# Windowed attention with an MLP on one core: shared places for the early pairs, a modelled short transfer queue, and GpSimd waits on VectorE

## The chip, the core and the metric

One of the eight cores of a Trainium2 chip. A core has TensorE (PE: matmuls into PSUM), VectorE (DVE), ScalarE (ACT), GpSimd (POOL), SyncE (SP, which issues the DMAs here) and 16 DMA engines. The metric is the device time of one execution in microseconds. Three runs of the kernel before took 712.12, 712.63 and 714.5 us, so their median is 712.63.

## The reference

```python
# q, k, v: 4 batches x 8 heads x 768 x 64; n_global 8, n_local 96
scores = q @ k.T / 8
rel = i - j;  local = (0 <= rel < n_local);  globl = j < n_global
dist = where(globl & ~local, n_local, abs(rel))
scores = where(local | globl, scores - slope[head] * dist, -1e9)
a = softmax(scores);  x = (a @ v), heads side by side     # 3072 x 512
h = x @ w_in                                              # 512 x 2048
out = (h * cos(h)) @ w_out                                # 2048 x 512
```

Inputs are float32, but the two weight matrices arrive as 64-bit floats, twice as many bytes.

## The kernel before, in words

**Tiles.** The 3072 tokens are 8 chunks of 384 (`CW`). Attention goes by chunk and pair of heads: 32 units, each with one transfer of queries and keys (`raw`), one of values (`v`, in two DMAs), score matmuls, folds and minima on VectorE (lines 538, 547), exponentials on ScalarE (572), sums and reciprocals (580, 583), norms (595, 600), transposes on TensorE (664), masks into `pv` (672, 677) and the product with the values (699), whose result is split into a high and a low part `xh`, `xl` (720). The first 8 units (`EXACT`) score in float32 straight from `raw`; the others split queries and keys into two parts each (`qs`, `ks`: lines 619, 623, 257 or 255, 632). The running extreme of the scores is kept by line 563.

**MLP.** It has 128 steps, one for each chunk and each of 16 slices of 128 hidden columns. A step has 12 matmuls (735), the angle and cosine (752 on ScalarE, 755 on VectorE, 758 on ScalarE), the product h*cos(h) (793), its split into `gh` and `gl` (253, 255 or 257; 802), and nine matmuls of the second product (746). The steps run in the order of `PHASES`: chunk 0 with slices 0 to 7, chunk 1 with all 16, chunk 0 with slices 8 to 15, then the other chunks.

**Weights.** Each of the 32 slices of 512 KB is turned from 64-bit to 32-bit floats once: low word (378 or 380), sign (385 on VectorE or 388 on GpSimd), bias (394 or 396), join (399, VectorE), high part (`w`), rest (409). Many of these may run on one of two or three engines.

**Order.** A planner (`Plan.run`) writes out the order of all engines ahead of time. Each operation has a list of engines with a cost in ns, the operations that it comes after, the places (`Slot`) that it uses, and a due time. The planner steps through its own time, gives each free engine the ready operation with the earliest due time whose places are free, and so fixes engine, order and buffer of each. Each engine then executes its instructions in this order. Two things of its model matter here. GpSimd's operations and those of VectorE marked `port=True` (among them 385, 399, 409, 563, 580, 583, 595, 600, 623, 632, 802 and the copies) hold one common port (`self.port`), so in the plan they never overlap; folds, minima and reads of PSUM aren't marked. Nothing in the emitted program holds an engine to its turn at the port: an instruction waits for its data and places alone. The other is SyncE, which issues a transfer 0.47 us after the last one, however many are still under way; the time of the transfers is modelled as one queue (`dma`), in which each starts behind the last.

**Places.** A class of places is a list of buffer names (`tt` 5, `st` 3, `v` 3, `pv` 3, `raw` 3, `qk` 2). The place of a split pair, `qk`, is a pair of tiles `q0`, `k0` or `q1`, `k1`, in use from the ninth unit on.

**Fillers.** In `emit`, matmuls of zeros (1039) fill planned gaps of TensorE up to 45 us.

Of the kernel before, what the change touches and what calls it, by code (L numbers as in the profile page):

```python
# [10 lines left out]
F32 = mybir.dt.float32  # L11
# [40 lines left out]
PIECES = {-1: [(0, 128), (128, 384)]}  # L52
NT, NST, NPV, NX, NV, NRAW, NQK, NRR, NG = 5, 3, 3, 2, 3, 3, 2, 3, 2

EXACT = 8

FILL_TO, FILL_REST, FILL_EACH, FILL_FIRST, FILL_COLD = 45000, 150, 250, 10, 7000
# [29 lines left out]
class Plan:  # L87
# [38 lines left out]
    def run(self):  # L126
# [19 lines left out]
        while todo:  # L146
# [5 lines left out]
            while again:  # L152
                again = False
                for e, f in self.free.items():
# [55 lines left out]
                    if e == SP:  # L210
                        dma = max(end + 300, dma) + o.extra
                        end = dma + 1400
                    out.append(o)
# [19 lines left out]
class Net:  # L233
# [26 lines left out]
    def constants(self):  # L260
# [7 lines left out]
        make_identity(nc, self.ident)  # L268
        tile3 = lambda name, **kw: self.const.tile([R, 3, SLOT], F32, name=name, **kw)


        self.dd = tile3("dd")
        self.tmp = [tile3(f"tmp{i}", tag=f"tt{i}") for i in range(3)]
        rel, col, _ = self.tmp
# [148 lines left out]
    def plan_loads(self, n, b2):  # L423
# [6 lines left out]
        lead = 1 if c == 0 else 0  # L430
        vs = Slot("v", lambda i: self.work.tile([SLOT, 1 + CT, W], F32, name="v", tag=i))
        L = dict(n=n, first=c == 0, v=vs)
# [18 lines left out]
    def chain(self, name, o):  # L451

        prev = self.prev.get(name)
        if prev is not None:
            o.after.append(prev)
            prev.then.append(o)
            o.left += 1
        self.prev[name] = o
        return o

    def bank(self, cls="att"):
        return Slot(cls, lambda i: self.psum.tile([P, 512], F32, name="bank", tag=i))

    def plan_unit(self, L, pr):
# [13 lines left out]
        if exact:  # L478
# [14 lines left out]
            ready = [p.op({ACT: 520, DVE: 300, POOL: 490}, queries, [o], [raw], port=True)]  # L493
            heads = [(raw, ready)] * 2
        else:
# [4 lines left out]
        st = u["st"] = Slot("st", lambda i: self.work.tile([R, 6 * CT], F32, name="st", tag=i))  # L500
        tt = u["tt"] = [Slot("tt", lambda i: self.const.tile([R, 2, 2, SLOT], F32, name="tt", tag=i)) for _ in range(0, CT, 2)]
        lead = lambda t: first and t == 0
# [4 lines left out]
        for js, h in [(js, h) for js in (((0, 1),) if exact else ((0,), (1,))) for h in range(0, CT, 2)]:  # L507
# [4 lines left out]
            def score(e, ts=ts, pss=pss):  # L512
                for i, t in enumerate(ts):
# [3 lines left out]
                    for j, ps in pss.items():  # L517
                        out = ps.tile[:R, i * WIN : i * WIN + w]
                        if exact:
                            z = raw.tile[j * D : (j + 1) * D]  # L520
                            nc.tensor.matmul(out, z[:, KW:][:, q0], z[:, k : k + w], start=True, stop=True)
                            continue
                        qs, ks = heads[j][0].tile
                        for m in range(2):
# [5 lines left out]
                {PE: cost}, score, [o for j in js for o in heads[j][1]],  # L530
                list(pss.values()) + [heads[j][0] for j in js[:1]] + [st, tt[h // 2]], mode="rows" if exact else None,
            ))
# [74 lines left out]
    def plan_split(self, raw, src, k0, sc):  # L607

        nc, p, D = self.nc, self.plan, self.D
        qk = Slot("qk", lambda i: [  # L610
            self.work.tile([P, 2, CW], F32R, name="qs", tag=f"q{i}"),
            self.work.tile([P, KW], F32R, name="ks", tag=f"k{i}"),
        ])

# [3 lines left out]
        def qhigh(e):  # L618
            nc.scalar.activation(qk.tile[0][:, 0], raw.tile[:, KW:], AF.Copy, scale=sc)

        def qrest(e):
            qs = qk.tile[0]
            nc.vector.scalar_tensor_tensor(  # L623
                qs[:, 1], raw.tile[:, KW:], sc, qs.bitcast(F32)[:, 0], op0=ALU.mult, op1=ALU.subtract
            )

        def khigh(e):
            self.copy(e, qk.tile[1][:, k0:], raw.tile[:, k0:KW])

        def krest(e):  # L630
            ks = qk.tile[1]
# [6 lines left out]
        q = self.chain("qhigh", p.op({ACT: 410}, qhigh, loads, [raw, qk]))  # L638
        q = p.op({DVE: 470}, qrest, [q], [raw, qk], port=True)
        k = self.chain("khigh", p.op(  # L640
            {ACT: 50 + w * 427 // 512, DVE: 70 + w * 265 // 512, POOL: 100 + w * 490 // 512},
            khigh, loads, [raw, qk], port=True,
        ))
        k = p.op({DVE: 70 + w * 535 // 512, POOL: 100 + w * 1125 // 512}, krest, [k], [raw, qk], port=True)
        return qk, [q, k]

    def plan_values(self, u):
# [5 lines left out]
        for h in range(0, CT, 2):  # L653
            pt = self.bank(att)

            pv = Slot("pv", lambda i: self.work.tile([P, 2, 4 * R], F32, name="pv", tag=i))
            lead = u["first"] and h == 0
# [331 lines left out]
    def windows(self):  # L989
# [7 lines left out]
                "px": banks[6:8], "early": banks[5:8] + banks[0:5], "pxearly": banks[6:8] + banks[2:5],  # L997
                "tt": names("tt", NT), "st": names("st", NST), "qk": names("qk", NQK), "raw": names("raw", NRAW),
                "v": names("v", NV), "pv": names("pv", NPV), "x": names("x", NX),
                "rr": names("rr", NRR), "gg": names("gg", NG), "wu": names("wu", 2), "part": names("part", NTOK),  # L1000
# [22 lines left out]
    def emit(self, ops, banks):  # L1023
# [3 lines left out]
        for u in {id(u): u for o in ops for u in o.uses if u.at in held}.values():  # L1027
            held[u.at].append((u.begin, u.end))
        last = 0
        for o in ops:  # L1030
            if o.engine == PE and o.start < FILL_TO:
# [67 lines left out]
```

## Time and profile before

| | us |
|---|---|
| median of the runs | 712.63 |
| the profiled execution: time | 714.17 |
| its span in the trace | 712.4 |
| TensorE matmul busy | 688.6 (97%) |
| VectorE busy | 518.8 (73%) |
| ScalarE busy | 450.9 (63%) |
| GpSimd busy | 135.8 (19%) |

Shares over the span hide that it has two parts. In the first 100 us or so the weights are brought in and converted beside the attention of two chunks; then TensorE works almost without a stop up to 705 us. Busy time of TensorE includes fillers. Busy time of VectorE includes time in which an instruction that has started waits for something that the profile doesn't show. The names DVE, ACT, POOL, PE and SP in rows are those of the engines above; `raw`, `wu` and `w` with 128x512 are weights, `tt` and `st` scores and their statistics.

### The profile page before, as it was taken

What the parts mean: (1) busy time and instruction counts of PE and PEld (TensorE: products, weight loads), DVE (VectorE), ACT (ScalarE), POOL (GpSimd) and SP (SyncE); (2) the same over time, 40 slices, a digit from 0 to 9 for tenths busy, and PEclk for the clock granted to TensorE, in tenths of its full rate; (3) what the DMA queues carried; (4) which work ended last, traced back from release to release, by engine and by line L of the source; (5) the groups of instructions that cost most, each with busy time, mean ns of one, the idle gap of its engine ahead of it and who ended that gap; (6) DMA issues with size and microseconds to landing.
All of it is one profiled execution on the core that took longest, in us unless ns stands there. A gap on an engine that the chain in (4) does not pass through costs nothing.

```text
span 712.4 us, 12947 instructions
## 1 busy us (share of the span) xinstructions
PE 688.6 (97%) x4483; PEld 598.4 (84%) x4483; DVE 518.8 (73%) x1542; ACT 450.9 (63%) x1130; POOL 135.8 (19%) x166
## 2 busy tenths in 40 slices
PE   7898999999999999999999999999999999999996
PEld 3657878988888888889889898888888888899884
DVE  7999999898767778487775887667785877743332
ACT  5799977786756576466664667566764666634342
POOL 4715656530002121011000121011000112000000
PEclk8999999999999999999999999999999999999999
DMA  8997210022420322132230422203122310001001
GB/s 303 407 351 209 59 48 24 1 59 64 112 68 29 83 65 65 48 103 60 56 71 15 112 61 58 59 19 106 42 68 67 90 49 2 1 1 45 1 0 50
DMA packets 32603, 55.74 MB, mean 78 GB/s; under 512 B 3472, under 2 KB 18192, under 8 KB 32528
## 3 DMA queue, kind: packets, MB, share of 16 engines
q1 hardware_dynamic: 32528, 54.82, 26.4%
q8 instruction: 37, 0.61, 0.4%
q14 instruction: 38, 0.31, 0.1%
HBM read 48.52 MB, written 6.29 MB: 77 GB/s over the span
## 4 chain that ended last, share of the span: by engine, by line
PE 72%; DVE 11%; ACT 8%; issue 2%; DMA 1%; POOL 0%; ACTq 0%; DVEq 0%; POOLq 0%; SPq 0%
PE bank L735 31%; PE bank L746 30%; PE bank L699 5%; PE bank L525 3%; ACT tt L572 2%; PE bank L664 2%; DVE wu L399 1%; ACT rr L758 1%; ACT L572 1%; DVE w L409 1%; DVE tt L547 1%; DVE gl L802 1%; DVE rr L755 1%; DVE qs L623 1%; DMA raw<-in_qk_dram 1%
## 5 line engine op out<-in xcount | busy, mean ns | idle before, releaser
L735 PE MATMUL bank<-xh,w 128*128 128x384 f32 x1024 | 298.1, 343 | 4.3 <-DVE rr L793 4.3
L746 PE MATMUL bank<-w,gh 128*128 128x512 f32 x768 | 243.6, 398 | 0.0
L735 PEld LDWEIGHTS bank<-xh,w 128*128 128x128 f32 x1024 | 189.1, 189 | 12.0 <-DVE rr L793 5.8
L735 PE MATMUL bank<-xl,w 128*128 128x384 f32 x512 | 173.3, 339 | 0.8 <-DVE xl L720 0.8
L746 PEld LDWEIGHTS bank<-w,gh 128*128 128x128 f32 x768 | 138.4, 188 | 21.5 <-ACT raw L394 0.3
L746 PE MATMUL bank<-w,gl 128*128 128x512 f32 x384 | 151.9, 396 | 0.0
L755 DVE SCALAR_TENSOR_TENSOR rr<-rr,bank 128x384 f32<-128x384 int32 x129 | 69.8, 542 | 102.6 <-ACT rr L752 102.2
L752 ACT ACTIVATE rr<-bank 128x384 int32<-128x384 f32 x129 | 62.1, 482 | 127.5 <-PE bank L735 124.5
L758 ACT ACTIVATE rr<-rr,half_pi 128x384 f32<-128x384 f32 x129 | 78.4, 613 | 43.0 <-DVE rr L755 41.4
L735 PEld LDWEIGHTS bank<-xl,w 128*128 128x128 f32 x512 | 96.8, 189 | 5.4 <-DVE xl L720 1.4
L793 DVE TENSOR_TENSOR rr<-bank,rr 128x384 f32<-128x384 f32 x129 | 70.5, 551 | 41.2 <-ACT rr L758 40.6
L572 ACT ACTIVATE tt<-tt,st 96x104 f32<-96x104 f32 (+1 forms) x256 | 94.2, 369 | 7.0 <-DVE st L547 6.4
L746 PEld LDWEIGHTS bank<-w,gl 128*128 128x128 f32 x384 | 72.1, 188 | 16.7
L257 POOL TENSOR_SCALAR ks<-raw 128x408 fp32r<-128x408 f32 (+1 forms) x35 | 21.1, 602 | 308.6 <-PE bank L525 291.6
L802 DVE TENSOR_TENSOR gl<-rr,gh 128x384 fp32r<-128x384 f32 (+1 forms) x113 | 65.9, 583 | 7.7 <-ACT gh L253 5.5
L253 ACT CAST gh<-rr 128x384 fp32r<-128x384 f32 (+1 forms) x99 | 50.2, 508 | 29.0 <-DVE rr L793 20.5
L547 DVE CUSTOM_DVE_ANT_0 tt<-bank,dd 96x104 f32<-96x104 f32 (+1 forms) x256 | 55.7, 257 | 3.0
L699 PEld LDWEIGHTS bank<-pv,v 104*64 104x64 f32 (+1 forms) x960 | 42.1, 138 | 12.5 <-issue 8.0
L525 PEld LDWEIGHTS bank<-ks,qs 128*96 128x96 f32 x384 | 45.8, 162 | 5.3 <-issue 0.8
L699 PE MATMUL bank<-pv,v 104*64 104x96 f32 (+1 forms) x960 | 48.3, 252 | 0.8 <-DMA raw<-in_qk_dram 0.4
L525 PE MATMUL bank<-ks,qs 128*96 128x200 f32 (+1 forms) x384 | 47.9, 255 | 0.5 <-DVE st L547 0.5
L572 ACT ACTIVATION_READ_ACCUMULATOR tt<-tt,st 96x1 f32 x256 | 47.9, 187 | 0.0
(96 smaller groups left out, 727.0 us busy)
## 6 DMA issues: line engine op xcount, KB each, us to landing
raw<-in_qk_dram SPq DMA_DIRECT2D x48, 224.0 KB
raw<-in_qk_dram SPq DMA_DIRECT2D x48, 198.0 KB
raw<-in_w_in_dram SPq DMA_DIRECT2D x16, 512.0 KB
raw<-in_w_out_dram SPq DMA_DIRECT2D x16, 512.0 KB
out_dram<-oo SPq DMA_DIRECT2D x24, 256.0 KB
v<-in_v_dram SPq DMA_DIRECT2D x16, 240.0 KB
v<-in_v_dram SPq DMA_DIRECT2D x16, 192.0 KB
raw<-in_qk_dram SPq DMA_DIRECT2D x4, 448.0 KB
```

The lines of the kernel that those rows point to most:

```text
L253: self.nc.scalar.copy(out, x)
L525: nc.tensor.matmul(out, qs[:, m, q0], ks[:, k : k + w], start=m == 0, stop=m == 1)
L547: nc.vector.tensor_tensor_reduce(tt[t // 2].tile[:, t % 2, j, :w], ps.tile[:R, i * WIN : i * WIN + w], self.dd[:, v, :w], op0=ALU.add, op1 ...
L572: nc.scalar.activation(x, x, AF.Exp, bias=st.tile[:, c : c + 1], scale=-1.0, accum_out=st.tile[:, n2 + c : n2 + c + 1])
L699: nc.tensor.matmul(px.tile[j * D : (j + 1) * D, t * R : (t + 1) * R], vs.tile[:k, t + c, hs][:, j * D : (j + 1) * D], pv[:k, c, o : o + R] ...
L735: self.nc.tensor.matmul(ph[:, :CW], self.wi[f][:, w, kk * P : (kk + 1) * P], xx[:, kk, :], start=kk == 0 and m == 0, stop=kk == self.NK - ...
L746: self.nc.tensor.matmul(po, gg[:, ts], self.wo[f][:, w, :], start=start and m == 0, stop=stop and m == 2)
L752: self.nc.scalar.activation(r.bitcast(I32), ph, AF.Copy, scale=1.0 / TWO_PI, bias=0.25)
L755: self.nc.vector.scalar_tensor_tensor(r, r.bitcast(I32), -TWO_PI, ph, op0=ALU.mult, op1=ALU.add)
L758: self.nc.scalar.activation(r, r, AF.Sin, bias=self.half_pi)
L793: {DVE: dve}, lambda e, r=r, h=h: nc.vector.tensor_tensor(r(), h(), r(), op=ALU.mult), [o], [ph, rr]
L802: self.eng(e).tensor_tensor(g[1][:, cs], r(), g[0].bitcast(F32)[:, cs], op=ALU.subtract)
```

## The change

Four edits, all in the planner and what it is given, with some counts:

1. The first seven units (`HOMES`) take `tt`, `v` and `pv` from longer lists of places: `ttearly` has `k0` and `k1` besides, `vearly` has `q0`, `pvearly` has `q1`. For that the pair of tiles `qk` becomes two classes, `q` and `k`. `NST` goes from 3 to 5.
2. In the plan SyncE is free for the next transfer only when the modelled queue is at most `DEPTH` = 3000 ns ahead. The program has no such wait; it changes which transfer is chosen next, and so the order.
3. In `emit`, the first GpSimd operation behind a port operation of VectorE (in the order of the plan) gets a dependency on the last instruction of that operation.
4. The tiles `tmp` and `tt` come from another pool, with the same names and sizes.

```diff
-NT, NST, NPV, NX, NV, NRAW, NQK, NRR, NG = 5, 3, 3, 2, 3, 3, 2, 3, 2
+NT, NST, NPV, NX, NV, NRAW, NQK, NRR, NG = 5, 5, 3, 2, 3, 3, 2, 3, 2
+
+DEPTH = 3000
...
+HOMES = 7
...
                     if e == SP:
                         dma = max(end + 300, dma) + o.extra
+
+                        self.free[SP] = max(end, dma - DEPTH)
+                        heapq.heappush(heap, self.free[SP])
                         end = dma + 1400
...
-        vs = Slot("v", lambda i: self.work.tile([SLOT, 1 + CT, W], F32, name="v", tag=i))
+        vs = Slot(self.early("v", n, b2), lambda i: self.work.tile([SLOT, 1 + CT, W], F32, name="v", tag=i))
...
+    def early(self, cls, n, pr):
+
+        return f"{cls}early" if n * self.NP + pr < HOMES else cls
...
-        tt = u["tt"] = [Slot("tt", lambda i: self.const.tile([R, 2, 2, SLOT], F32, name="tt", tag=i)) for _ in range(0, CT, 2)]
+        tt = u["tt"] = [
+            Slot(self.early("tt", n, pr), lambda i: self.work.tile([R, 2, 2, SLOT], F32, name="tt", tag=i))
+            for _ in range(0, CT, 2)
+        ]
...
-        qk = Slot("qk", lambda i: [
-            self.work.tile([P, 2, CW], F32R, name="qs", tag=f"q{i}"),
-            self.work.tile([P, KW], F32R, name="ks", tag=f"k{i}"),
-        ])
+        qq = Slot("q", lambda i: self.work.tile([P, 2, CW], F32R, name="qs", tag=i))
+        kk = Slot("k", lambda i: self.work.tile([P, KW], F32R, name="ks", tag=i))
...
-            pv = Slot("pv", lambda i: self.work.tile([P, 2, 4 * R], F32, name="pv", tag=i))
+            pv = Slot(self.early("pv", n, pr), lambda i: self.work.tile([P, 2, 4 * R], F32, name="pv", tag=i))
...
-                "v": names("v", NV), "pv": names("pv", NPV), "x": names("x", NX),
+                "v": names("v", NV), "pv": names("pv", NPV), "ttearly": names("tt", NT) + names("k", 2),
+                "vearly": names("v", NV) + ["q0"], "pvearly": names("pv", NPV) + ["q1"], "x": names("x", NX),
...
+        held_by = None
+        behind = mybir.DependencyInfo(mybir.DependencyClass.Sync, mybir.DependencyReason.SCHED_ONLY)
         for o in ops:
...
+            new = len(nc.cur_bb.bb.instructions)
             o.emit(o.engine)
+            if o.engine in (DVE, POOL):
+                engine = self.eng(o.engine).engine
+                new = [i for i in nc.cur_bb.bb.instructions[new:] if i.engine == engine]
+                if o.engine == DVE and o.port:
+                    held_by = new[-1]
+                elif o.engine == POOL and held_by is not None:
+                    self.tc.add_manual_dep(new[0], held_by.name, behind, reason="port")
+                    held_by = None
```

Lines of the changed kernel are numbered 6 to 13 higher from the planner on (399 is 405, 600 is 613, 755 is 766).

GpSimd, at its first conversions of weights, with buffer numbers (`raw_120` to `raw_124` are weights, `tt_258` and `tt_326` scores of the second and third unit) and the semaphores that each row waits for. Before:

```order
32 L380 TENSOR_SCALAR raw_120<-raw_120 128x512 [waits DMAHW1_49]
33 L388 TENSOR_SCALAR raw_120<-raw_120 128x512 [waits Pool_49]
34 L595 TENSOR_TENSOR tt_258<-tt_258,st_259 96x2x96 [waits DVE_49,Activation_49]
35 L595 TENSOR_TENSOR tt_258<-tt_258,st_259 96x208 [waits Activation_49]
36 L388 TENSOR_SCALAR raw_122<-raw_122 128x512 [waits DMAHW3_49,Activation_49]
37 L380 TENSOR_SCALAR raw_124<-raw_124 128x512 [waits DMAHW4_49]
38 L490 TENSOR_SCALAR raw_229<-raw_229,steep_104 128x384 [waits DMAHW6_49,PE_49]
39 L388 TENSOR_SCALAR raw_124<-raw_124 128x512 [waits Pool_49]
40 L396 TENSOR_SCALAR raw_124<-raw_124 128x512 [waits Pool_49]
```

After:

```order
32 L386 TENSOR_SCALAR raw_120<-raw_120 128x512 [waits DMAHW1_49,DVE_49]
33 L394 TENSOR_SCALAR raw_120<-raw_120 128x512 [waits Pool_49]
34 L608 TENSOR_TENSOR tt_258<-tt_258,st_259 96x2x96 [waits DVE_49,Activation_49]
35 L608 TENSOR_TENSOR tt_258<-tt_258,st_259 96x208 [waits Activation_49]
36 L386 TENSOR_SCALAR raw_122<-raw_122 128x512 [waits DMAHW6_49,DVE_49]
37 L394 TENSOR_SCALAR raw_122<-raw_122 128x512 [waits Pool_49]
38 L402 TENSOR_SCALAR raw_122<-raw_122 128x512 [waits Pool_49]
39 L608 TENSOR_TENSOR tt_326<-tt_326,st_327 96x2x96 [waits DVE_49,Activation_49]
40 L608 TENSOR_TENSOR tt_326<-tt_326,st_327 96x208 [waits Activation_49]
41 L394 TENSOR_SCALAR raw_124<-raw_124 128x512 [waits DMAHW7_49,DVE_49,Activation_49]
```

The rows that follow VectorE's port operations have gained `DVE_49`, VectorE's semaphore; the norms of the third unit have come to GpSimd, and the conversions are in another order.

SyncE, where the values of the fourth unit stand. Before (the first row of `v` is theirs):

```order
18 L372 DMA raw<-in_w_in_dram 128x1024
19 L372 DMA raw<-in_w_out_dram 128x1024
20 L372 DMA raw<-in_w_in_dram 128x1024
21 L372 DMA raw<-in_w_out_dram 128x1024 x3
22 L483 DMA raw<-in_qk_dram 128x896
23 L372 DMA raw<-in_w_out_dram 128x1024
24 L372 DMA raw<-in_w_in_dram 128x1024 x2
25 L438 DMA v<-in_v_dram 96x4x128
26 L441 DMA v<-in_v_dram 8x3x128
```

After (the second `v` of 96 rows is theirs):

```order
7 L444 DMA v<-in_v_dram 96x4x128
8 L378 DMA raw<-in_w_in_dram 128x1024
9 L493 DMA raw<-in_qk_dram 128x792
10 L447 DMA v<-in_v_dram 8x3x128
11 L444 DMA v<-in_v_dram 96x4x128
12 L447 DMA v<-in_v_dram 8x3x128
13 L378 DMA raw<-in_w_in_dram 128x1024 x3
14 L378 DMA raw<-in_w_out_dram 128x1024
15 L493 DMA raw<-in_qk_dram 128x896
```

The values and the next queries and keys have moved ahead of the weights; weights and transfers of units now alternate all the way.

VectorE, ahead of its first angle. Before:

```order
170 L563 TENSOR_TENSOR worst<-worst,st 96x8
171 L385 TENSOR_SCALAR raw<-raw 128x512
172 L720 TENSOR_TENSOR xl<-bank,xh 128x384
173 L538 COPY_PREDICATED bank<-mine,bank 96x2x96
174 L672 TENSOR_TENSOR pv<-bank,others 104x384
175 L677 TENSOR_TENSOR pv<-bank,own 96x384
176 L538 COPY_PREDICATED bank<-mine,bank 96x2x96
177 L755 SCALAR_TENSOR_TENSOR rr<-rr,bank 128x384
```

After:

```order
134 L560 ISA tt,st<-bank,dd 96x104
135 L560 ISA st 96x1
136 L415 TENSOR_TENSOR w<-wu,w 128x512
137 L405 SCALAR_TENSOR_TENSOR wu<-raw 128x512
138 L766 SCALAR_TENSOR_TENSOR rr<-rr,bank 128x384
139 L551 COPY_PREDICATED bank<-mine,bank 96x2x96 x2
```

The first angle has moved from row 177 to row 138; weights (415, 405) stand right ahead of it where masks of another unit (672, 677) stood.

## Rows read from the trace of the kernel before

**Rows 1.** Windows: stretch, length, busy us (instructions) of each engine, granted clock, DMA.

```profile
10.00:57.00 47.00, 37.16 (x288) 23.63 (x289) 45.53 (x171) 38.73 (x122) 21.28 (x22) 0.93 1.04 385
57.00:100.00 43.00, 42.94 (x325) 36.21 (x326) 40.62 (x109) 38.72 (x92) 27.53 (x24) 0.96 0.33 83
155.00:600.00 445.00, 441.91 (x2945) 393.50 (x2944) 327.37 (x1019) 282.02 (x721) 51.44 (x64) 1.00 0.24 63
```

**Rows 2.** Windows, filler matmuls of line 1039 alone.

```profile
10.00:57.00 47.00, 13.90 (x55) 5.01 (x55) 0.93 1.04 385
```

**Rows 3.** Timeline of VectorE at the ninth angle: start, us, what.

```profile
104.40 1.01 DVE L755 SCALAR_TENSOR_TENSOR rr<-rr,bank 128x384 f32<-128x384 int32 x2
```

**Rows 4.** Groups of VectorE by form, 10 to 100 us: busy us, mean ns.

```profile
L399 DVE SCALAR_TENSOR_TENSOR wu<-raw 128x512 uint32<-128x512 uint32 x17 | 12.8, 762 | 0.0
L600 DVE TENSOR_TENSOR tt<-tt,st 96x416 f32<-96x416 f32 x11 | 9.6, 892 | 0.0
L409 DVE TENSOR_TENSOR w<-wu,w 128x512 fp32r<-128x512 f32 x10 | 7.6, 765 | 0.0
L563 DVE TENSOR_TENSOR worst<-worst,st 96x8 f32<-96x8 f32 x8 | 3.3, 409 | 0.0
L580 DVE TENSOR_SCALAR st<-st 96x8 f32<-96x8 f32 x8 | 2.9, 367 | 0.6 <-ACT tt L572 0.5
```

**Rows 5.** Lines of VectorE: durations ns min/median/max (409 over the whole span).

```profile
L399 DVE SCALAR_TENSOR_TENSOR wu<-raw x17: 673/681/1550, 24.7 to 97.3; 128x512 uint32<-128x512 uint32 x17
L600 DVE TENSOR_TENSOR tt<-tt,st x11: 575/580/1746, 12.3 to 93.6; 96x416 f32<-96x416 f32 x11
L409 DVE TENSOR_TENSOR w<-wu,w x17: 656/678/1572, 31.3 to 155.3; 128x512 fp32r<-128x512 f32 x17
L563 DVE TENSOR_TENSOR worst<-worst,st x8: 111/262/1039, 17.7 to 89.9; 96x8 f32<-96x8 f32 x8
L580 DVE TENSOR_SCALAR st<-st x8: 156/206/720, 10.8 to 91.4; 96x8 f32<-96x8 f32 x8
```

**Rows 6.** Timeline of GpSimd and VectorE at 12 us.

```profile
12.20 1.33 POOL L388 TENSOR_SCALAR raw<-raw 128x512 bf16<-128x512 bf16 x1
12.27 1.44 DVE L600 TENSOR_TENSOR tt<-tt,st 96x416 f32<-96x416 f32 x1
```

**Rows 7.** Timeline of VectorE and GpSimd at 86 us: a wait of GpSimd.

```profile
85.69 0.68 DVE L399 SCALAR_TENSOR_TENSOR wu<-raw 128x512 uint32<-128x512 uint32 x1
86.45 0.62 POOL L257 TENSOR_SCALAR w<-wu 128x512 fp32r<-128x512 f32 x1 [0.85 <-DVE wu L399]
```

**Rows 8.** Timeline of SyncE and TensorE, 28 to 57 us.

```profile
28.70 0.33 SPq L438 DMA_DIRECT2D v<-in_v_dram  x1
39.32 1.31 PE L521 MATMUL bank<-raw 64*96 64x200 f32 x8
48.99 1.39 PE L699 MATMUL bank<-pv,v 96*64 96x96 f32 x28
56.84 0.44 PE L735 MATMUL bank<-xh,w 128*128 128x384 f32 x1 [3.70 <-DVE rr L793]
```

**Rows 9.** Timeline of VectorE, 36 to 41 us: from start to start.

```profile
36.20 0.74 DVE L385 TENSOR_SCALAR raw<-raw 128x512 uint16<-128x512 uint16 x1
36.73 0.58 DVE L720 TENSOR_TENSOR xl<-bank,xh 128x384 fp32r<-128x384 f32 x1
39.59 1.28 DVE L399 SCALAR_TENSOR_TENSOR wu<-raw 128x512 uint32<-128x512 uint32 x2
```

**Rows 10.** Timeline of VectorE and GpSimd at 313 us.

```profile
313.13 1.84 DVE L623 SCALAR_TENSOR_TENSOR qs<-raw,qs 128x384 fp32r<-128x384 f32 x2
313.50 1.06 POOL L802 TENSOR_TENSOR gl<-rr,gh 128x384 fp32r<-128x384 f32 x1 [4.17 <-ACT gh L253]
```

**Rows 11.** Line 623 over the span.

```profile
L623 DVE SCALAR_TENSOR_TENSOR qs<-raw,qs x48: 520/546/1372, 103.3 to 599.2; 128x384 fp32r<-128x384 f32 x48
```

**Rows 12.** Waits of SyncE's queue, 0 to 110 us: us in total, times, longest.

```profile
SPq L616 <- DVE qs L623: 45.0, 3, 38.6
```

More of the change, by code (lines that the diff above doesn't have):

```diff
@@ L268, in constants @@
         make_identity(nc, self.ident)
-        tile3 = lambda name, **kw: self.const.tile([R, 3, SLOT], F32, name=name, **kw)
-        self.dd = tile3("dd")
-        self.tmp = [tile3(f"tmp{i}", tag=f"tt{i}") for i in range(3)]
+        self.dd = self.const.tile([R, 3, SLOT], F32, name="dd")
+        self.tmp = [self.work.tile([R, 3, SLOT], F32, name=f"tmp{i}", tag=f"tt{i}") for i in range(3)]
         rel, col, _ = self.tmp
@@ L493, in plan_unit @@
             ready = [p.op({ACT: 520, DVE: 300, POOL: 490}, queries, [o], [raw], port=True)]
-            heads = [(raw, ready)] * 2
+            heads = [([raw], ready)] * 2
         else:
@@ L522, in score @@
                             continue
-                        qs, ks = heads[j][0].tile
+                        qs, ks = [x.tile for x in heads[j][0]]
                         for m in range(2):
@@ L530, in plan_unit @@
                 {PE: cost}, score, [o for j in js for o in heads[j][1]],
-                list(pss.values()) + [heads[j][0] for j in js[:1]] + [st, tt[h // 2]], mode="rows" if exact else None,
+                list(pss.values()) + heads[js[0]][0] + [st, tt[h // 2]], mode="rows" if exact else None,
             ))
@@ L618, in qhigh @@
         def qhigh(e):
-            nc.scalar.activation(qk.tile[0][:, 0], raw.tile[:, KW:], AF.Copy, scale=sc)
+            nc.scalar.activation(qq.tile[:, 0], raw.tile[:, KW:], AF.Copy, scale=sc)
         def qrest(e):
-            qs = qk.tile[0]
+            qs = qq.tile
             nc.vector.scalar_tensor_tensor(
@@ L627, in khigh @@
         def khigh(e):
-            self.copy(e, qk.tile[1][:, k0:], raw.tile[:, k0:KW])
+            self.copy(e, kk.tile[:, k0:], raw.tile[:, k0:KW])
         def krest(e):
-            ks = qk.tile[1]
+            ks = kk.tile
             self.eng(e).tensor_tensor(
@@ L637, in plan_split @@
         w = KW - k0
-        q = self.chain("qhigh", p.op({ACT: 410}, qhigh, loads, [raw, qk]))
-        q = p.op({DVE: 470}, qrest, [q], [raw, qk], port=True)
+        q = self.chain("qhigh", p.op({ACT: 410}, qhigh, loads, [raw, qq]))
+        q = p.op({DVE: 470}, qrest, [q], [raw, qq], port=True)
         k = self.chain("khigh", p.op(
             {ACT: 50 + w * 427 // 512, DVE: 70 + w * 265 // 512, POOL: 100 + w * 490 // 512},
-            khigh, loads, [raw, qk], port=True,
+            khigh, loads, [raw, kk], port=True,
         ))
-        k = p.op({DVE: 70 + w * 535 // 512, POOL: 100 + w * 1125 // 512}, krest, [k], [raw, qk], port=True)
-        return qk, [q, k]
+        k = p.op({DVE: 70 + w * 535 // 512, POOL: 100 + w * 1125 // 512}, krest, [k], [raw, kk], port=True)
+        return [qq, kk], [q, k]
     def plan_values(self, u):
@@ L997, in windows @@
                 "px": banks[6:8], "early": banks[5:8] + banks[0:5], "pxearly": banks[6:8] + banks[2:5],
-                "tt": names("tt", NT), "st": names("st", NST), "qk": names("qk", NQK), "raw": names("raw", NRAW),
-                "v": names("v", NV), "pv": names("pv", NPV), "x": names("x", NX),
+                "tt": names("tt", NT), "st": names("st", NST), "q": names("q", NQK), "k": names("k", NQK), "raw": names("raw", NRAW),
+                "v": names("v", NV), "pv": names("pv", NPV), "ttearly": names("tt", NT) + names("k", 2),
+                "vearly": names("v", NV) + ["q0"], "pvearly": names("pv", NPV) + ["q1"], "x": names("x", NX),
                 "rr": names("rr", NRR), "gg": names("gg", NG), "wu": names("wu", 2), "part": names("part", NTOK),
```

## The prediction

> **What bounds the kernel now.** I read the stretches first. They give each engine's busy time in five parts of the span, and the reader is to see that the limit changes. From 155 to 600 us TensorE is busy 441.91 of 445 us and VectorE 327.37; nothing but TensorE's own work can be shortened there, apart from a few stops. From 10 to 57 us TensorE is busy 37.16 of 47 us, while VectorE is busy 45.53, and from 57 to 100 us VectorE still has 40.62 of 43 [rows 1]. TensorE's 37.16 us hold 13.90 us of the filler matmuls of line 1039 [rows 2], so 23.3 of those 47 us are work and 23.7 us are free. The DMA engines are full in the first of these stretches too (385 GB/s, against 83 in the second), but VectorE is idle for only 1.5 us of it, so it is not kept waiting by them. The engine that the others wait for in the ramp is VectorE. It reaches the ninth angle (line 755, the first step of the second chunk) at 104.40 us [rows 3] with 3.9 us of idle since 10 us.
>
> Next I read VectorE's groups by form for 10 to 100 us, beside the quiet length of the same instructions. They say that VectorE's busy time is partly waiting: the mean of line 399 is 762 ns against a median of 681, of line 600 892 against 580, of line 409 765 against 678, of line 563 409 against a shortest of 111, of line 580 367 against 156 [rows 4, 5]. Over their counts that is 17x81 + 11x312 + 10x87 + 8x298 + 8x211 ns = 1.4 + 3.4 + 0.9 + 2.4 + 1.7 = 9.8 us. The timeline shows what does it: a VectorE norm of line 600 that starts at 12.27 takes 1.44 us, because GpSimd's line 388 has started at 12.20 and takes 1.33 [rows 6]. An operation of 0.1 us (line 563) can lose 0.9 us in this way.
>
> **The GpSimd waits.** The order shows 89 of GpSimd's 147 instructions behind a VectorE semaphore, where it was 41 of 133. The planner never lets two port operations overlap, so a VectorE port operation that stretches over a GpSimd one met a GpSimd operation that ran ahead of its place, or stood behind one that was planned before it. VectorE has hardly any idle time in the ramp, which a planned wait for the port would have left room for, and GpSimd is busy only 21.28 of 47 us [rows 1], so it is the one that runs ahead. I expect most of the 9.8 us to go. What comes instead: a GpSimd operation that waits starts 0.08 us after VectorE's end (line 399 ends at 86.37, line 257 starts at 86.45 [rows 7]), and queued behind it on GpSimd stand the other conversions of weights, for which ScalarE and then VectorE's joins (line 399) wait. If each of the 46 GpSimd operations between 10 and 100 us [rows 1] passes that 0.08 us on to VectorE, the waits cost 3.7 us and remove nothing; if the stretching goes wholly and hidden lateness costs nothing, they give 9.8. I take 7, nearer to the row of the stretches, since GpSimd has idle time to absorb lateness.
>
> On the collision itself the row says that VectorE's norm ended at 13.71, 0.18 us behind GpSimd's end at 13.53 [rows 6]. The Trainium skill (SBUF — State Buffer, section "Who interferes with whom") says that an operation which finds the shared port taken blocks fully until the holder is done, and that issue order decides who blocks. By full blocking the norm would have ended at 13.53 + 0.58 = 14.11; the trace has 0.4 us less, so I go by the measured stretches. That issue order decides agrees with the rows, and it also speaks against the change: it is the second rival below.
>
> **The places and the order of transfers.** The order moves the values of the fourth pair. Before, SyncE issued them at 28.70 us, its products on TensorE (line 699) came at 48.99 us, and the third step's matmuls started only at 56.84, after 3.7 us of idle that a VectorE multiplication (line 793) ended [rows 8]. After, that transfer stands behind one weight transfer instead of 18, and the first angle of VectorE (766, was 755) stands at row 138 instead of 177. So the first chunk's steps start earlier, and the free 23.7 us of TensorE begin to fill. But VectorE must do the steps' work instead of something else, so I count what lies ahead of the ninth angle in both orders: four fewer of line 385, three fewer of line 399, and ten small differences more. With the pace from start to start (line 385: 36.20 to 36.73, so 0.53; line 399: two in 1.28 us of which one is 0.68, so 0.60 [rows 9]) the first two are 4x0.53 + 3x0.60 = 3.9 us, and all differences together 5.8. The four conversions go to GpSimd, where each takes about 1.33 us [rows 6], with room for it. None of this work is gone: the weights come later in VectorE's order, at a time in which TensorE has become the limit. I therefore take 2.5 of the 5.8, with bounds of 0 and 5.8. The extra places (tt, v, pv in those of the split pairs; two more st) add no instruction. The number of fillers falls from 65 to 30, which removes nothing that waits.
>
> **The steady stretch.** At 313.13 us two operations of line 623 take 1.84 us, of which GpSimd's line 802, started at 313.50, causes the second one's length of 1.37 [rows 10]; the median of the line is 0.55, the longest 1.37 [rows 11]. The pattern occurs three times with over 0.8 us (146.81, 313.6, 480.4). TensorE is already the limit there and gets the score's queries late. With the wait behind the second 623 this loss of 3x0.82 = 2.5 us can go; I take 2.0, bounds 0 and 2.5.
>
> **The sum.** 7 + 2.5 + 2.0 = 11.5 us. The profiled execution took 714.17 us (span 712.4), so it would take 702.7; it stands 1.54 over the median of the runs shown, 712.63. The forecast for the median is 701.1. The bounds are +3.7 - 0 - 0, which is 716.3, and -9.8 - 5.8 - 2.5 = -18.1, which is 694.5. TensorE's 23.7 free us leave room for the largest gain.
>
> **Rivals.**
> 1. The stretches only change sides. VectorE's next operation starts as its predecessor ends, 0.08 us before the waiting GpSimd sees it [rows 7], and takes the port again; GpSimd comes late, and VectorE's joins then wait for the weights of GpSimd. For it: the many back-to-back port operations in the ramp. Against it: between them stand the folds, minima and PSUM reads (lines 538, 547, 672, 677, 755, 793), which aren't marked as port operations and give GpSimd its turn. Then the first term is about 0 and the rest 4.5: 708.1.
> 2. GpSimd becomes the chain. By issue order GpSimd loses every turn it has waited for, and 24 operations between 57 and 100 us, with 27.53 us of busy time [rows 1], each come one VectorE operation (0.5 us) late: 12 us, which eat the whole 11.5. Then the time is that of before, 713. GpSimd's idle time speaks against it.
> 3. Slower: SyncE's queue. Now 20 of the 32 weight transfers stand behind the transfer of the eighth pair, which needs the place that the fifth pair's second scoring frees. Before, a transfer of this kind waited 38.6 us, with no weight behind it [rows 12]. In before that scoring is not done until 40.6 us [rows 8]; issued at 41, 20x512 KB at 385 GB/s [rows 1] take 27 us and land up to 68 us, where the full stretch ended at 57 [rows 1]. If VectorE, which takes its instructions in order, comes to their joins first, it idles for those 11 us, and for some 4 more where the later transfers of queries and values, which stand between the weights, wait for their places: 15 us against the 11.5 of the gain, so 716. It decides if VectorE idles over 12 us between 35 and 80 us. Against it: those weights are joined late in the new order, and steps of the second half of the weights start after 120 us.
> 4. More than forecast: all three terms at their upper bounds, 694.5, if VectorE's order really is the only limit of the ramp.
>
> **How the numbers follow.** The forecast gets 0.62, rival 1 0.20, rival 2 0.05, rival 3 0.08, rival 4 0.05. The forecast's own range is 697 to 706. I take 694 to 710, which holds the forecast, rival 4 and most of rival 1, and leaves out rivals 2 and 3 and some of rival 1's side above 710. About 0.3% (2.1 us) is what a measurement of this kernel can tell from no change. Faster by more: 0.62 + 0.20 + 0.05 = 0.87; the same: 0.05; slower: 0.08.
>
> **What would show it.** In the profile after, lines 576, 593, 613, 405 (were 563, 580, 600, 399) between 10 and 100 us have means within 0.1 us of the quiet lengths; GpSimd's waits name VectorE; VectorE's ninth angle (766) starts 8 to 12 us before 104.40; line 634 (623) has no length over 1 us at the places in the steady stretch; and the fourth group of values on TensorE (line 710) comes before 38 us. The forecast is wrong if the ninth angle comes at 100 us or later, if VectorE is idle for over 8 us between 10 and 80 us, or if TensorE after 155 us has more idle time than the 3.1 us of now.

## The result, and the profile after

The changed kernel takes 705.59 us (median of 4 runs, 704.92 to 706.55) against 712.38 for the kernel before beside it (4 runs). The ratio is 0.990, 95% interval 0.9876 to 0.9924: a gain of 7.1 us by the ratio and 6.8 by the medians, where 11.5 were forecast. A later repetition gave 0.9901 (0.9878 to 0.9925). The two profiled executions are 714.17 and 704.92 us, a long one of the kernel before and the shortest of the changed kernel, so their difference of 9.2 us holds about 2 us of chance.

Windows of the changed kernel, with the columns of [rows 1]:

```profile
10.00:57.00 47.00, 40.83 (x329) 30.22 (x328) 43.67 (x182) 41.18 (x133) 26.41 (x28) 0.89 0.95 310
57.00:100.00 43.00, 38.19 (x283) 32.43 (x283) 40.40 (x99) 41.40 (x92) 25.94 (x23) 1.00 0.56 168
155.00:600.00 445.00, 442.74 (x2961) 393.65 (x2960) 324.48 (x999) 277.59 (x701) 52.09 (x68) 1.00 0.24 63
```

And the fillers (line 1054, was 1039) in the first stretch:

```profile
10.00:57.00 47.00, 5.00 (x20) 1.70 (x20) 0.89 0.95 310
```

TensorE's 40.83 us hold 5.00 of fillers, so it is busy with work for 35.8 us between 10 and 57 us where it was for 23.3 [rows 1, 2], at a mean granted clock of 0.89 instead of 0.93. It is idle for 4.8 us in the second stretch, where it had no idle time to speak of: the work has been drawn forward, and some of what was won is given back there. Between 155 and 600 us it is idle for 2.3 us (3.1 before). VectorE is idle for 5.9 us between 10 and 100 us, where it was for 3.9.

Groups of VectorE by form between 10 and 100 us, as in [rows 4], with one line more:

```profile
L405 DVE SCALAR_TENSOR_TENSOR wu<-raw 128x512 uint32<-128x512 uint32 x18 | 12.8, 719 | 0.0
L415 DVE TENSOR_TENSOR w<-wu,w 128x512 fp32r<-128x512 f32 x13 | 10.9, 835 | 0.3 <-ACT w L260 0.2
L613 DVE TENSOR_TENSOR tt<-tt,st 96x416 f32<-96x416 f32 x11 | 6.9, 649 | 0.0
L593 DVE TENSOR_SCALAR st<-st 96x8 f32<-96x8 f32 x8 | 2.0, 248 | 0.3 <-ACT tt L585 0.3
L576 DVE TENSOR_TENSOR worst<-worst,st 96x8 f32<-96x8 f32 x8 | 1.5, 183 | 0.0
L813 DVE TENSOR_TENSOR gl<-rr,gh 128x384 fp32r<-128x384 f32 x7 | 5.5, 788 | 0.2 <-ACT gh L260 0.2
```

The quiet lengths over the whole span (columns as in [rows 5]; 593 and 576 have their shortest at 156 and 110 ns):

```profile
L405 DVE SCALAR_TENSOR_TENSOR wu<-raw x32: 633/680/1372, 26.9 to 153.5; 128x512 uint32<-128x512 uint32 x32
L415 DVE TENSOR_TENSOR w<-wu,w x19: 673/693/1342, 28.6 to 152.6; 128x512 fp32r<-128x512 f32 x19
L613 DVE TENSOR_TENSOR tt<-tt,st x39: 577/581/1135, 11.5 to 604.9; 96x416 f32<-96x416 f32 x39
```

By the sum of the prediction (count times mean less quiet length) the five forms now lose to stretches (time beyond the quiet length) 18x39 + 13x142 + 11x68 + 8x92 + 8x73 ns = 4.6 us, where they lost 9.8. So 5.2 us went; in the trace of the repetition (f0 below) the same sum is 5.5, so about 1 us of this is chance. The sum leaves out line 813 (was 802), whose median over the span is 558 ns: it loses 1.6 us now and lost 0.8 before, in this line:

```profile
L802 DVE TENSOR_TENSOR gl<-rr,gh 128x384 fp32r<-128x384 f32 x4 | 3.0, 758 | 0.2 <-ACT gh L253 0.2
```

GpSimd's waits between 10 and 100 us (what waited, for whom: us in total, times, longest):

```profile
POOL raw L394 <- DVE wu L405: 7.3, 4, 2.6
POOL raw L394 <- DVE w L415: 5.3, 4, 2.4
POOL raw L386 <- DVE tt L613: 4.5, 2, 4.0
```

The longest of them name VectorE's port operations. On VectorE's timeline the ninth angle (second row) and the one before it:

```profile
87.97 0.56 DVE L766 SCALAR_TENSOR_TENSOR rr<-rr,bank 128x384 f32<-128x384 int32 x1
90.58 0.54 DVE L766 SCALAR_TENSOR_TENSOR rr<-rr,bank 128x384 f32<-128x384 int32 x1
```

The ninth comes 13.8 us before that of [rows 3]. On TensorE's timeline the values of the fourth unit (line 710, was 699), 18.2 us before theirs in [rows 8]:

```profile
30.80 1.43 PE L710 MATMUL bank<-pv,v 96*64 96x96 f32 x26
```

From the 13th step on, the first matmuls of a step stand 8.6 to 10.5 us apart in the two traces, mostly 9.0 to 10.0, and 9.3 at the last step. So the ninth angle's 13.8 us were not all kept, and the long steady stretch added nothing.

### The profile page after: what moved, and what is told of

Same layout as the page of the kernel before. It is cut to its first block, busy times and chain, and to the rows that moved or that the text cites. A ratio compares the mean times of both kernels' runs of the same rounds, so it can differ in the third digit from the quotient of the medians.

```text
span 703.2 us, 12932 instructions
## 1 busy us (share of the span) xinstructions
PE 681.4 (97%) x4448; PEld 595.5 (85%) x4448; DVE 506.0 (72%) x1531; ACT 450.2 (64%) x1129; POOL 140.1 (20%) x180
## 5 line engine op out<-in xcount | busy, mean ns | idle before, releaser
L813 DVE TENSOR_TENSOR gl<-rr,gh 128x384 fp32r<-128x384 f32 (+1 forms) x114 | 67.9, 595 | 10.2 <-ACT gh L260 7.4
L264 POOL TENSOR_SCALAR ks<-raw 128x408 fp32r<-128x408 f32 (+1 forms) x34 | 19.4, 570 | 273.7 <-PE bank L538 204.7
L710 PEld LDWEIGHTS bank<-pv,v 104*64 104x64 f32 (+1 forms) x960 | 42.6, 140 | 12.2 <-issue 7.7
```

Source lines behind the costliest of these rows:

```text
L710: nc.tensor.matmul(px.tile[j * D : (j + 1) * D, t * R : (t + 1) * R], vs.tile[:k, t + c, hs][:, j * D : (j + 1) * D], pv[:k, c, o : o + R] ...
L813: self.eng(e).tensor_tensor(g[1][:, cs], r(), g[0].bitcast(F32)[:, cs], op=ALU.subtract)
```

## The experiments

Two theories stood at the start. A: the gain is the port's turn, which GpSimd's waits (edit 3) keep. B: it is the new order (edits 1 and 2), which brings the first chunk's work forward. All runs together; the ratio is to the kernel before beside them, and "us" is (ratio - 1) x 712. VectorE's busy time and instructions between 10 and 155 us are from the windows.

| kernel | median | ratio (95%) | us | VectorE 10 to 155 us |
|---|---|---|---|---|
| before | 712.0 to 714.1 | 1 | 0 | 135.91 us, x375 |
| changed | 705.59 | 0.990 (0.9876 to 0.9924) | -7.1 | 132.04, x397 |
| f0: changed, once more | 706.85 | 0.9901 (0.9878 to 0.9925) | -7.0 | 132.36, x397 |
| e1: before + waits | 707.01 | 0.9916 (0.9901 to 0.9931) | -6.0 | 130.74, x400 |
| e2: changed, no waits | 716.85 | 1.0048 (1.003 to 1.0066) | +3.4 | 136.55, x361 |
| e3: places, no waits | 717.36 | 1.0076 (1.0052 to 1.01) | +5.4 | 136.49, x375 |
| e4: queue, no waits | 713.98 | 1.0024 (1.0003 to 1.0046) | +1.7 | 136.79, x367 |
| e7: places + waits | 703.96 | 0.9875 (0.9852 to 0.9897) | -8.9 | 135.98, x413 |
| e8: queue + waits | 703.25 | 0.9857 (0.9833 to 0.9881) | -10.2 | 130.75, x408 |
| e5: waits to 160 us only | 706.93 | 0.9914 (0.9894 to 0.9935) | -6.1 | 131.99, x398 |
| e6: behind any operation | 723.67 | 1.0145 (1.0122 to 1.0168) | +10.3 | 128.43, x366 |
| f2: waits both ways | 714.13 | 1.0008 (0.9994 to 1.0022) | +0.6 | 113.83, x367 |
| f4: e8 + handover in the plan | 701.78 | 0.9829 (0.9809 to 0.985) | -12.2 | 132.21, x410 |
| f3: changed + handover | 705.68 | 0.9918 (0.9892 to 0.9943) | -5.8 | 129.73, x402 |

**The parts by themselves: e1, e2.** e1 is the kernel before with edit 3 alone, e2 the changed kernel without it.

```diff
...
+                if o.engine == DVE and o.port:
+                    held_by = new[-1]
+                elif o.engine == POOL and held_by is not None:
+                    self.tc.add_manual_dep(new[0], held_by.name, behind, reason="port")
+                    held_by = None
```

> The kernel before with the GpSimd waits alone (edit 3), its own order and places. Theory A (GpSimd out of its turn at the port is what lengthens the ramp): VectorE's stretches between 10 and 100 us fall from about 12 us to under 5, and the time falls by 5 to 7 us, to 706 to 707. Theory B (the new order of places and transfers makes the gain, and it also removes the collisions): the time stays within 1.5 us of 712.4.

> The changed kernel without the GpSimd waits: places and order of transfers alone. Theory A: VectorE keeps about 12 us of stretches between 10 and 100 us and the time is 2 to 3 us under that of before, 709.5 to 710.5. Theory B: the time is that of the whole change, 705 to 707.

e1 measured 0.9916: theory A holds. e2 measured 1.0048, which neither theory allowed: the order alone makes the kernel slower. Groups of VectorE in e2, 10 to 100 us (lines of the changed kernel):

```profile
L405 DVE SCALAR_TENSOR_TENSOR wu<-raw 128x512 uint32<-128x512 uint32 x17 | 14.5, 860 | 0.0
L613 DVE TENSOR_TENSOR tt<-tt,st 96x416 f32<-96x416 f32 x11 | 9.2, 858 | 0.0
L415 DVE TENSOR_TENSOR w<-wu,w 128x512 fp32r<-128x512 f32 x11 | 8.4, 762 | 0.0
L593 DVE TENSOR_SCALAR st<-st 96x8 f32<-96x8 f32 x8 | 5.2, 652 | 0.0
L576 DVE TENSOR_TENSOR worst<-worst,st 96x8 f32<-96x8 f32 x8 | 2.9, 361 | 0.0
```

And in e1, in the lines of the kernel before:

```profile
L399 DVE SCALAR_TENSOR_TENSOR wu<-raw 128x512 uint32<-128x512 uint32 x19 | 13.2, 701 | 0.0
L409 DVE TENSOR_TENSOR w<-wu,w 128x512 fp32r<-128x512 f32 x11 | 7.7, 703 | 0.3 <-ACT w L253 0.3
L600 DVE TENSOR_TENSOR tt<-tt,st 96x416 f32<-96x416 f32 x11 | 6.8, 640 | 0.0
L580 DVE TENSOR_SCALAR st<-st 96x8 f32<-96x8 f32 x8 | 1.6, 196 | 1.4 <-ACT tt L572 1.4
L563 DVE TENSOR_TENSOR worst<-worst,st 96x8 f32<-96x8 f32 x8 | 1.2, 144 | 0.0
```

The sum over the five forms is 12.8 us in e2 (17x180 + 11x277 + 11x69 + 8x496 + 8x251 ns) and 1.9 in e1, against 9.8 before and 4.6 in the changed kernel. The instruction of line 593 shows it best: 0.16 us long when it is left alone, 0.65 on average in e2. Between e2 and the changed kernel, which have the same order and differ by the waits alone, 8.2 us of stretch go and 10.5 us of time. The granted clock doesn't tell these kernels apart: over the span it is 0.990 to 0.991 in e1's executions, 0.984 to 0.990 in the changed kernel's (both measurements), 0.987 to 0.990 in e2's and 0.987 to 0.994 in those of before beside e1.

The windows say the same by what VectorE gets done. From 10 to 155 us, first e2 and then the changed kernel:

```profile
10.00:155.00 145.00, 126.47 (x865) 103.20 (x865) 136.55 (x361) 116.23 (x296) 84.11 (x74) 0.95 0.51 163
```

```profile
10.00:155.00 145.00, 133.81 (x924) 111.47 (x923) 132.04 (x397) 125.41 (x323) 80.86 (x76) 0.96 0.53 163
```

36 instructions more in 4.5 us less. The last column of the table parts the kernels in two groups without an exception: 397 to 413 instructions by 155 us in those under 0.992 of before, 361 to 375 in the others. TensorE's matmuls by then part them as well (924 to 963 against 864 to 907), so such a count tells how far the ramp has come and not by itself which engine holds it up.

**Places and queue apart: e3, e4, e7, e8.** e3 is e2 without the `DEPTH` lines, e4 the kernel before with these lines alone. e7 is the changed kernel without them, and e8 is it with no shared places (it keeps five `st`).

```diff
-                        self.free[SP] = max(end, dma - DEPTH)
-                        heapq.heappush(heap, self.free[SP])
```

```diff
-HOMES = 7
+HOMES = 0
```

> The kernel before with the shared places alone (edits 1 and 4): transfers are still sent as early as SyncE can, no waits. Theory A: 0 to 2 us under before (710.5 to 712.5), since weights still stand ahead of the fourth unit's values in the queue. Theory B: if the places are what matters, 3 us or more under before.

> The kernel before with the modelled short queue alone (edit 2). Theory A: 1 to 2.5 us under before (710 to 711.5): it moves values and queries ahead of weights, but they wait for places. Theory B: 3 us or more under before.

> The changed kernel without the modelled short queue: the shared places and the waits alone. Without the waits this order took 717.36. Theory A, that the waits take away what VectorE loses in its stretched operations before 110 us, 13.1 us in the trace of that order, down to the 5 to 7 us that were left in the two orders with waits: 6 to 8 us, so 709.5 to 711.5. Theory B, that the waits are worth more in a new order whatever it is (11.3 us in that of the change): 705.5 to 707. Theory C, that the waits are worth what they were in the old order, 5.4: 712.

> The changed kernel with no shared places (HOMES = 0): the modelled short queue, the five st and the waits alone. Without the waits the order with the short queue took 713.98, with 15.0 us of stretched VectorE operations before 110 us. Theory A, that the waits leave 5 to 7 of these: 8 to 10 us, so 704 to 706. Theory B, that the shared places are what makes the new order pay: at least the 707.0 of the old order with waits, 707 to 709.

Without the waits both orders are slower than before, by 5.4 and 1.7 us, where all four theories of e3 and e4 had a gain or no change. With the waits e8 is 3.1 us better than the change as a whole; the intervals just touch (0.9881 against 0.9876), but the change was measured twice with the same ratio. e7 is 1.8 us better, which is within the noise. The waits are worth 6.0 us in the old order, 14.3 with the places (e3 to e7), 11.9 with the queue (e4 to e8, which also has the two more `st`) and 10.5 with both (e2 to changed). So they are worth more in each new order, as theory B of e7's expectation had it, though e7's 703.96 is still under its 705.5. For e8 theory A is the nearer one (703.25 against 704 to 706), and B falls.

One thing isn't explained by the stretches: in e3 the five forms lose 8.4 us, less than in the kernel before, VectorE's busy time and count are those of before (136.49, x375), and yet the median is 5.4 us later. The trace shows little of it: it is of e3's shortest execution (715.59 us), which stands 1.4 us behind the profiled one of before. The others go up to 721.29; the two longest had a granted clock of 0.982 over the span, where the others had 0.986 to 0.991. What lowered it there was not traced.

**Waits in the steady stretch: e5.**

```diff
-                elif o.engine == POOL and held_by is not None:
+                elif o.engine == POOL and held_by is not None and o.start < 160000:
```

> The changed kernel with GpSimd's waits only for operations planned before 160 us of the plan's time; in the steady stretch GpSimd runs freely again. The three collisions of line 634 (1.37 us) come back. Theory A, that a removed collision in the steady stretch is worth its stretch: 0.5 to 0.8 us each, so 707.1 to 708.0 against 705.59. Theory B, that the waits cost in the steady stretch as much as they remove, since the drift between the two traces after 200 us was +0.7 us and not -2: 704.5 to 705.6.

It measured 0.9914 against 0.9900 (706.93 us, between the ranges of the two theories); the intervals overlap, so 1 us is the size to expect, not a proof. The traces agree with theory A's direction. Line 634 from 155 to 600 us, first in e5 and then in the changed kernel:

```profile
L634 DVE SCALAR_TENSOR_TENSOR qs<-raw,qs x44: 519/547/1370, 156.1 to 592.8; 128x384 fp32r<-128x384 f32 x44
```

```profile
L634 DVE SCALAR_TENSOR_TENSOR qs<-raw,qs x44: 518/545/881, 155.6 to 589.9; 128x384 fp32r<-128x384 f32 x44
```

Two collisions of about 1.37 us come back, near 305 and 472 us. The third one, before 155 us, had not gone: the whole span of the changed kernel has

```profile
L634 DVE SCALAR_TENSOR_TENSOR qs<-raw,qs x48: 518/545/1326, 101.9 to 589.9; 128x384 fp32r<-128x384 f32 x48
```

and its longest, 1.33 us, stands at 139 us, where the kernel before had 1.37 at 146.81 us. Where each of the two goes away (near 303 and 470 us), TensorE's steps come 0.5 us earlier, not 0.82. Over the whole steady stretch e5's steps fall behind by 2.6 us against the trace of the changed kernel and by 1.7 against that of f0, so the waits may do more there than remove these two; the runs don't show what.

**GpSimd behind any VectorE operation: e6.**

```diff
-                if o.engine == DVE and o.port:
+                if o.engine == DVE:
```

> The changed kernel with GpSimd's first operation behind the last VectorE operation of any kind in the plan, not only behind one that uses the port. Theory A, that the waits are paid out of GpSimd's idle time: 705 to 707. Theory B, that a wait costs what it makes GpSimd late and GpSimd's lateness reaches VectorE's joins of weights: a fold or minimum of 0.25 to 0.55 us later at each of some 50 operations of the ramp, of which half reaches VectorE, so 5 us or more: 710 to 714.

1.0145, beyond both theories. TensorE's waits after 155 us, first in e6, then in the changed kernel:

```profile
PE bank L675 <- POOL tt L613: 6.1, 6, 1.6
```

```profile
PE bank L675 <- POOL tt L613: 1.1, 3, 0.6
```

And GpSimd's norms of line 613 in the same stretch, first in e6, then in the changed kernel:

```profile
L613 POOL TENSOR_TENSOR tt<-tt,st x8: 877/1624/1627, 228.5 to 620.8; 96x416 f32<-96x416 f32 x8
```

```profile
L613 POOL TENSOR_TENSOR tt<-tt,st x8: 877/877/878, 218.8 to 604.7; 96x416 f32<-96x416 f32 x8
```

Five of these eight take 1.62 us. One of them on the timelines of GpSimd and VectorE in e6:

```profile
264.57 1.62 POOL L613 TENSOR_TENSOR tt<-tt,st 96x416 f32<-96x416 f32 x1 [2.59 <-DVE rr L766]
```

```profile
263.98 0.50 DVE L766 SCALAR_TENSOR_TENSOR rr<-rr,bank 128x384 f32<-128x384 int32 x1
264.40 0.58 DVE L613 TENSOR_TENSOR tt<-tt,st 96x416 f32<-96x416 f32 x1
264.90 1.70 DVE L634 SCALAR_TENSOR_TENSOR qs<-raw,qs 128x384 fp32r<-128x384 f32 x2
```

In the changed kernel this norm starts behind a reciprocal (596), while VectorE runs the angle (766), which isn't marked as a port operation and beside which the norm keeps its 0.88 us. In e6 it waits for the angle too, and VectorE's own norm has started 0.17 us before it. GpSimd's norm then takes 1.62 us, the second of the two operations of line 634 1.23, and TensorE's transposes (675) wait. This is rival 1's mechanism, made by a wait behind the wrong operation: GpSimd's turn was the time of the angle. These waits are about 5 of the 16 us between the two traces; 8 us are lost before the 25th step (171 us in e6), and what loses them was not taken apart.

**Waits both ways: f2, and the change once more: f0.** Same order to the last instruction; VectorE's port operations also wait for the GpSimd operation planned before them.

```diff
                 if o.engine == DVE and o.port:
+                    if last_pool is not None:
+                        self.tc.add_manual_dep(new[0], last_pool.name, behind, reason="port")
+                        last_pool = None
                     held_by = new[-1]
```

(`last_pool` is the last instruction of GpSimd's latest operation.)

> The changed kernel once more, beside the two next kernels. Theory A, that with the waits either new order alone is better than both together: it stays at 705.6, 0.990 of before, over 2 us behind the kernel without shared places (703.25). Theory B, that the distance came from different chips in different sessions: 703 to 704.

> The changed kernel, in the same order to the last instruction, with waits the other way too: VectorE's first port operation behind a GpSimd operation (in the order of the plan) waits for it. In the changed kernel VectorE still loses 6.8 us before 110 us in stretched operations, where it runs ahead of a late GpSimd. Theory A, that a stretch is only the remainder of the turn and a wait makes it an idle time of the same length: 705 to 707, the stretches near 0 and VectorE idle that much more. Theory B, that the collision itself slows both: 701 to 704. Theory C, that GpSimd is so late that VectorE pays the whole of its lateness: 708 to 712.

The stretches are gone. Of line 415 and 593 in f2, 10 to 100 us:

```profile
L415 DVE TENSOR_TENSOR w<-wu,w 128x512 fp32r<-128x512 f32 x11 | 7.6, 692 | 2.7 <-POOL raw L394 1.0 <-POOL w L415 0.5 <-POOL raw L386 0.5
L593 DVE TENSOR_SCALAR st<-st 96x8 f32<-96x8 f32 x8 | 1.3, 164 | 2.0 <-POOL w L415 1.0 <-ACT raw L498 0.7 <-POOL raw L402 0.3
```

But the time is that of the kernel before, 7.3 us over f0's 706.85: beyond even theory C. The window from 10 to 155 us:

```profile
10.00:155.00 145.00, 128.79 (x881) 106.18 (x878) 113.83 (x367) 118.13 (x300) 74.69 (x74) 0.95 0.51 163
```

VectorE's busy time falls by 18.2 us, it does 30 instructions fewer, and its waits for GpSimd come to some 20 us in this window, where the changed kernel shows none. The reading that fits: where it ran into a late GpSimd it lost the rest of that operation; where it waits, it idles until GpSimd has begun and ended, and for the handover. So stretches gone are no gain in themselves; it matters which engine waits in their place. f0 has the ratio of the first measurement, so the distance to e8 fits theory A and not a difference between chips.

**The handover in the plan: f4 and f3.** f4 is e8, f3 the changed kernel, with a planner that gives GpSimd the port 90 ns after a VectorE operation.

```diff
+HAND = 90
...
-                    held = self.port > t
+                    held = self.port + (HAND if e == POOL and self.last == DVE else 0) > t
...
```

(with the same sum where the planner compares engines, and f4 with e8's `HOMES = 0`.)

> The kernel without shared places (703.25), with a planner that knows the handover: GpSimd may take the port 90 ns after a port operation of VectorE, which is what the wait costs in the trace. So the planned start of GpSimd is no longer too early, and VectorE doesn't run into it. Theory A, that the stretches that were left (3.5 us before 110 us, some 6 later) come from the missing handover: half of them go, 700 to 702. Theory B, that each new order moves the ramp by some us whatever it models: 702 to 707.

> The changed kernel with the handover of 90 ns in the plan, the shared places kept: what made 701.78 of 703.25 without them. Theory A, that the handover is worth the same 1.5 us in any order: 0.988 of before, 704 to 705.5, and the shared places stay 2 to 3 us behind. Theory B, that the 1.5 us were the luck of one order: anywhere between 702 and 710.

f4 is the fastest kernel of the study: 701.78 us, 0.983 of before, which is in theory A's range. Its interval overlaps with e8's. Windows from 10 to 155 us, first f4, then e8:

```profile
10.00:155.00 145.00, 137.84 (x963) 112.80 (x965) 132.21 (x410) 128.52 (x330) 75.07 (x74) 0.99 0.52 166
```

```profile
10.00:155.00 145.00, 136.10 (x940) 111.73 (x937) 130.75 (x408) 124.37 (x324) 81.77 (x76) 0.96 0.52 165
```

Theory A's mechanism is not seen between 10 and 100 us: the five forms lose 3.6 us there, against 2.0 in e8. What differs is the granted clock, 0.99 against 0.96. Over the span it is 0.995 to 0.996 in f4's five executions and 0.989 to 0.995 in e8's, and the one of e8 at 0.995 took 702.0 us. So the clock is a rival for the whole of f4's step; as time and clock don't go together in the executions of before (711.87 us at 0.989, 714.03 at 0.991), it isn't shown either. The same edit on the changed kernel gives nothing (f3, 0.9918), which is theory B of its expectation. So whether f4's step is one order's luck, the clock's, or needs an order without shared places stays open.

## Why the prediction was right, and where its sizes were off

The direction and the main mechanism were right; that the median also falls inside the forecast's own range of 697 to 706 is in part luck, since 705.59 stands at its edge, the repetition's median is 706.85, and one of the three terms of the sum came out with the wrong sign by itself.

**What bounds the ramp** was right as far as the runs show. A change that adds no work and takes away VectorE's stretches moves the end (e1), and waits that make VectorE idle instead take the gain back (f2).

**Term 1, GpSimd's waits (-7).** That the waits make the gain is shown by e1 and by three more pairs that differ by them alone or nearly so (e2 and the changed kernel, e3 and e7, e4 and e8). Its size was too large for this order: 5.2 us of the 9.8 went (4.3 in the repetition), and four of the five lines came within 0.1 us of their quiet lengths; line 415 did not (835 against 693 ns), and line 813, which the sum had left out, lost more than before. e1 removed 7.9 of the 9.8 and gained 6.0 in the whole span. What is left fits VectorE running ahead into a late GpSimd, and f2 took it away at a loss.

**Term 2, order and places (-2.5).** This step failed as a step. It counted work that stands ahead of the ninth angle and held that to be independent of the waits. The ninth angle came 13.8 us earlier, more than the 8 to 12 forecast, and the fourth unit's values before 38 us as forecast. But the order alone costs 3.4 us (e2), beside more stretch (12.8 us against 9.8), and beside the waits it adds 1.1 us (0.9900 against 0.9916, with overlapping intervals). Of the 4.4 us that are missing by the ratio (11.5 - 7.1), this term has 1.4, term 1 has 1.8 by its stretches, and term 3 about 1.0 by e5's ratio; stretch and time are not the same, so this is a rough split, and the runs give no finer one.

**Term 3, the steady stretch (-2.0).** Of the three collisions of line 634 that it counted, two went; the one at 146.81 us stayed (1.33 us, now at 139 us). And a collision that loses 0.82 us on VectorE is worth 0.5 on TensorE, so the two give 1.0 us, as e5's ratio has it, though e5's trace has more. Between the 21st and the 49th step the new order gives 0.8 back. The sign "no length over 1 us" held after 155 us (0.88 at most), and TensorE's idle time between 155 and 600 us fell from 3.1 to 2.3 us.

**The rivals.** Rival 1 (stretches only change sides) fell: VectorE's stretches shrank, and between 10 and 155 us no wait of VectorE for GpSimd shows. Rival 2 (GpSimd becomes the chain) fell for this change, but e6 shows that it is near: one rule more for whom GpSimd waits, and the kernel is 17 us slower than the change. Rival 3 (SyncE's queue) fell: VectorE is idle for 4.4 us between 10 and 80 us, not over 8:

```profile
10.00:80.00 70.00, 59.01 (x483) 44.68 (x483) 65.64 (x249) 64.06 (x188) 40.23 (x42) 0.93 0.96 305
```

**Not settled:** why the queue alone is better than both orders together (-10.2 against -7.1; the -8.9 of the places alone is within the noise of the change), and why e3 is as slow as it is. In e8's trace the five forms lose 2.0 us where the changed kernel loses 4.6, but that execution is e8's longest (706.51 us) and longer than the changed kernel's profiled one (704.92), so the 2.6 us can't be set against the 3.1 us of the ratios. What makes GpSimd late in the one order and not in the other was not taken apart.

## What to carry to other kernels

When an order is planned on the ground that two engines never use a shared port at once, hold the engine with idle time to that plan; a new order without it can lose time where it plans to win some. Put the wait on the engine that is not the bound, and only behind operations that take the port: the same wait on the bound engine, or behind any neighbour, cost 7 and 17 us here. Judge parts of such a change in pairs, since their worths don't add, and watch how many instructions the engines have done by a fixed time, beside how long those were stretched.

## What the runs showed of the hardware

Two norms of the same kind that meet are not slowed alike. On the timelines of GpSimd and VectorE in the changed kernel:

```profile
271.75 0.88 POOL L613 TENSOR_TENSOR tt<-tt,st 96x416 f32<-96x416 f32 x1 [2.85 <-DVE st L596]
```

```profile
271.94 1.14 DVE L613 TENSOR_TENSOR tt<-tt,st 96x416 f32<-96x416 f32 x1
```

GpSimd, first by 0.19 us, keeps its 0.88 us, and VectorE ends 0.45 us behind it, with 0.58 as its quiet length: it had done little before. In e6 GpSimd is the second, behind a VectorE norm that ends 0.41 us after GpSimd's start and with two operations of line 634 close behind that, and takes 0.75 us more (1.62 against 0.88). The Trainium skill (SBUF — State Buffer, section "Who interferes with whom") says that the operation that comes second waits until the holder is done; for this pair the trace nearly agrees, 0.13 us short of it, where the pair of [rows 6] was 0.4 us short. And what a collision costs doesn't scale with the work of the operation that loses: in e2 an operation of 0.16 us (line 593) took 0.65 on average.
